# Moving start-up memsets, two loads and one copy in a fused strided-sparse attention and feed-forward kernel

## The chip, the cores and the metric

The kernel runs on one core of one Trainium2 chip. The metric is the device time of one execution in microseconds (us). A core has five engines that run their own instruction streams: TensorE (PE in the profile, its weight loads PEld), VectorE (DVE), ScalarE (ACT), GpSimd (POOL) and SyncE (SP, which here only issues transfers). Sixteen DMA engines move the data. GpSimd's loads go through the queue q0 of the profile, those of SyncE through q1, two of ScalarE's through q10.

## The reference

```python
# q, k, v: (batch 8, heads 8, seq 576, head_dim 64)
scores = (q @ k^T) / sqrt(64)
rel = pos[:, None] - pos[None, :]
local   = (rel >= 0) & (rel < 32)                       # heads 0 to 3
strided = (rel >= 0) & (pos_k % 32 == pos_q % 32)       # heads 4 to 7
attn = softmax(where(mask, scores, -1e9)) @ v
x = attn as (4608 tokens, 512)
h = x @ w_in                                            # (4608, 2048)
g = max(h, 0) + alpha * min(h, 0)                       # alpha per column of h
out = g @ w_out                                         # (4608, 512), float32
```

## The kernel before

The work of a batch is four *pairs* of heads: pairs 4b and 4b+1 are batch b's local heads, 4b+2 and 4b+3 its strided ones. A local pair is cut into six blocks of 96 queries against 128 keys, a strided pair into eight blocks of 72 by 72, because only positions with the same remainder attend to each other. For each pair `score_both` forms the scores on TensorE, ScalarE takes the exponential (L391, L400, L406), and GpSimd (for pair 11 VectorE) multiplies the mask in (L402, L409). `pv_piece` multiplies with V, whose 65th column of ones gives the sum of each row; VectorE takes its reciprocal (L437) and scales (L439) into a 16-bit tile x, for some strided pairs the fixed tile `x16s`. Then x is turned so that head dimensions lie on partitions, into `xT`, a ring of 1536 columns: either by TensorE (`x_piece`, L455, and a copy out of PSUM, L230 on ScalarE or L232 on VectorE) or by a DMA transpose from SyncE (`x_dma`: L472 for a local pair; L469 into `xs` for a strided one, which ScalarE then copies into `xT` at L478).

The feed-forward part works on nine chunks of 512 tokens. `lin1_piece(n, m)` multiplies one of 16 column blocks of w_in with chunk n (L613, four matmuls over the four pairs' 128 rows), ScalarE takes the negative part (L621), VectorE finishes the activation into `gT` (L624). `lin2_fast` is the second product (L709, L719) by seven products of halves instead of eight, for which sums of halves of g (`g_sum`, L653, on GpSimd or VectorE) and of w_out are formed. For chunk n, a loop of 30 steps i runs 16 steps of `lin1_piece` and 14 of `lin2_fast`; between them `attn_n` puts pieces of the attention of a later batch, taken from the list `pieces` in a fixed order. The step with the index g in that list has the scores of pair g, the products with V of pair g-1 and the turning of x of pair g-2; some of its pieces also cast or load the next batches' data. All instructions are kept in program order on each engine, so each engine's order is what this order of calls makes.

q and k of a batch's local heads reach SBUF as 32-bit tiles (`load_qk`, L104) and are cast to 16 bits (`cast_l`, L234 on GpSimd, L230 on ScalarE), then turned on TensorE (L292). From batch 5 on they come as rows (`load_rows`, L116) and are turned by DMA. The strided q and k come into `qsd` and `ksd` (`load_d`, L135) and are turned by DMA into `qT` and `kT` (`transpose_d`, L176). V comes by `load_v`: a local one straight into `vl` (L222), a strided one into `stv` (L212), from which `cast_v` copies it into `vs`. The weights come by `load_w` in four parts each (L762 for w_in into `win`, L758 for w_out).

At the start TensorE runs seventeen warm-up matmuls (L769) while the first loads run. VectorE and GpSimd set the constant parts of tiles with memsets; those of GpSimd stand before and after its first loads: two of `stv`, two of `vl`, four of `win`. The first three batches' pieces and chunk 0 are called from lists written out by hand; the loop described above begins with chunk 1.

Of the kernel before, what the change touches and what calls it, by code (L numbers as in the profile page):

```python
# [32 lines left out]
def kernel(  # L33
# [10 lines left out]
    nc = tc.nc  # L44
    keep = tc.keep_in_program_order
# [44 lines left out]
    x16s = cpool.tile([80, 1024], F16)  # L90
# [114 lines left out]
    def load_v(b, strided):  # L205


        if strided:
            st = spool.tile([128, 2048], F16, tag="v", bufs=2, name="stv")
            step = 2 if b == 0 else 4  # L210
            for h in range(0, 4, step):
                keep(nc.gpsimd.dma_start(  # L212
                    st[0:72, 512 * h : 512 * (h + step)].rearrange("p (h e) -> p h e", h=step),
                    v[b, 4 + h : 4 + h + step, :, :].rearrange("h (p t) d -> p h (t d)", t=8)))
            loaded[b] = st
        else:
            v16 = vls[b % 2]
            base = v[b, 0:1, 0:1, :]
            r0 = 32 if b < 2 else 0
            step = 12 if b == 0 else 24  # L220
            for c in range(0, 24, step):
                keep(nc.gpsimd.dma_start(  # L222
                    v16[r0:128, c : c + step, 0:64],
                    bass.AP(tensor=base.tensor, offset=base.offset + (96 * c - 32 + r0) * D,
                            ap=[[D, 128 - r0], [96 * D, step], [1, D]])))
            cast16[(b, False, "v")] = v16
# [271 lines left out]
    def X(g, eng=None):  # L498
        return lambda: x_piece(pairs[g], eng or ("act" if pairs[g].strided else "dve"))

    for g in range(7, npair + 2):
        c = g // 4
        a, p, t = g, g - 1, g + 1
        okA = 8 <= a < npair
        okP = 8 <= p < npair
        okT = 8 <= t < npair and t < 4 * NX and (t % 4 == 0 or t < 4 * DX and t % 2 == 0)
        nP = len(pairs[p].pgroups) if okP else 0
        seq = []
        if okA:
            seq.append(("S", lambda a=a: score_both(pairs[a])))  # L510
        if okP:
            seq.append(("P", Pv(p, 0)))
        if okT:
            seq.append(("T", T(t // 2, "q")))
        if 8 <= g - 2 < npair and not pairs[g - 2].xd:
            seq.append(("X", X(g - 2)))
        if okP:
            seq.append(("P", Pv(p, 1)))
        if okT:
            seq.append(("Tk", T(t // 2, "k")))  # L520
        if nP == 3:
            seq.append(("P", Pv(p, 2)))
        if g == 14:
            seq[0], seq[1] = seq[1], seq[0]
        if not seq:
            seq.append(("N", lambda: None))

        todo = [(c, pr) for pr in range(2)] if g % 4 == 0 and 8 < g < npair else []

        if g % 4 == 1 and 9 <= g and c + 1 < B:  # L530
            todo = [(c + 1, nm) for nm in "qk"]
        lastP = max([i for i, z in enumerate(seq) if z[0] == "P"], default=len(seq) - 1)
        nslots = [i for i, z in enumerate(seq) if z[0][0] != "S"] or list(range(len(seq)))
        for i, (kind, fn) in enumerate(seq):
            extra = []
            if todo and i in nslots:
                left = len([z for z in nslots if z >= i])
                cnt = -(-len(todo) // max(1, left))
                extra = [todo.pop(0) for _ in range(min(cnt, len(todo)))]

            def run(fn=fn, extra=extra, g=g, c=c, kind=kind, lastp=(i == lastP), first=(i == 0),
                    second=(i == min(1, len(seq) - 1))):
                fn()
                for b, pr in extra:
                    if pr in ("q", "k"):
                        if b == 3:
                            continue
                        if b < NX:
                            cast_l(b, pr)
                        if b + 1 < NX:  # L550
                            load_qk(b + 1, pr)
                        continue
                    if b == 3:
                        continue
                    cast_v(b, pr, "pool")
                    if pr == 1 and b + 1 < B:
                        load_v(b + 1, True)
                if first and g % 4 == 2 and NX <= c + 1 < B:
                    turn_rows(c + 1)
                if lastp and g % 4 == 3 and NX <= c + 2 < B:  # L560
                    load_rows(c + 2, "k")
                if lastp:
                    if 4 * DX <= g - 1 < npair and pairs[g - 1].xd:
                        x_dma(pairs[g - 1])
                    if g % 4 == 3 and DX < c + 1 < B:
                        transpose_d()
                    if g % 4 == 2 and DX < c and c + 1 < B:
                        load_d(c + 1)
                    if g % 4 == 1 and DX < c and c + 1 < B:
                        load_v(c + 1, False)  # L570
                    if g % 4 == 1 and NX <= c + 2 < B:
                        load_rows(c + 2, "q")
                if second and 4 * DX <= g - 3 < npair and pairs[g - 3].xd and pairs[g - 3].strided:
                    after.append(lambda: x_copy(pairs[g - 3]))
            feed(run, g - 2 if kind == "X" else -1)
# [180 lines left out]
    def load_w(c, second):  # L756
        if second:
            keep(nc.gpsimd.dma_start(  # L758
                wout16[:, 4 * c : 4 * c + 4, :],
                moe_w_out[512 * c : 512 * c + 512, :].rearrange("(kf p) c -> p kf c", p=128)))  # L760
        else:
            keep(nc.gpsimd.dma_start(  # L762
                win16[:, :, 512 * c : 512 * c + 512],
                moe_w_in[:, 512 * c : 512 * c + 512].rearrange("(kk p) c -> p kk c", p=128)))
# [25 lines left out]
    keep(nc.vector.memset(kTs[1], 0.0))  # L790
    for t in ets:
        keep(nc.vector.memset(t[:, 576:640], 0.0))
    keep(nc.vector.memset(kTs[0][:, :, 0:32], 0.0))
    keep(nc.vector.memset(kTs[0][:, :, 608:672], 0.0))
    for nm in "qk":
        keep(nc.vector.memset(qks[nm][64:80], 0.0))
    keep(nc.gpsimd.memset(x16s[64:80], 0.0))
    keep(nc.vector.tensor_copy(id32, ident[0:72, 0:72]))

    keep(nc.gpsimd.memset(vss[0][:, :, :, 64:65], 1.0))  # L800
    keep(nc.gpsimd.memset(vls[0][0:32, 0:1, 0:64], 0.0))
    keep(nc.gpsimd.memset(vls[0][:, :, 64:65], 1.0))
    load_v(0, True)
    load_v(0, False)
    for c in range(4):
        load_w(c, False)
    keep(nc.gpsimd.memset(vls[1][0:32, 0:1, 0:64], 0.0))
    keep(nc.gpsimd.memset(vls[1][:, :, 64:65], 1.0))
    keep(nc.gpsimd.memset(vss[1][:, :, :, 64:65], 1.0))
# [136 lines left out]
    for n in range(1, NCH):  # L946
        ab = attn_until(n + 1) if n + 1 < B else len(pieces)
        left = ab - pos["i"]
        acc = 0.0
        for i in range(30):  # L950
            if i < 16:
                lin1_piece(n, 8 * (i // 8) + 2 * (i % 4) + i % 8 // 4)
            else:
                lin2_fast(n, i - 16)
            held = []
            if n == 1 and i == 15:
                held.extend(late)
                late.clear()
            if n == 1:
                cnt = int(i > 12 or i in (0, 2, 4, 6, 9, 11))  # L960
            else:
                acc += left / (19.5 if n == B - 2 else 21) * (0.5 if i < 16 else 1.0)
                cnt = int(acc)
                acc -= cnt
            attn_n(cnt, ab)
            for fn in held:
                fn()
            if n == 2 and i == 8:
                load_v(4, True)
            for z, h, eng in {1: early, 2: sums2}.get(n, sums).get(i, ()):  # L970
                g_sum(n, z, h, eng)
            if n > 1:
                continue
            if i == 7:
                for pr in range(2):
                    cast_v(2, pr, "pool")
                    load_qk(4, "qk"[pr])
            if i == 4:
                load_v(3, True)
            if i == 15:  # L980
                load_v(3, False)
                load_d(3)
                cast_l(3, "q", "act")
            if i == 17:
                cast_l(3, "k", "act")
            if i == 24:
                for pr in range(2):
                    cast_v(3, pr, "pool")
        while pos["i"] < ab:
            attn_step(ab)  # L990
# [30 lines left out]
```

## Time and profile before

| | |
|---|---|
| runs | 295.78, 296.0, 297.6 us; median 296.0 |
| profiled execution | 297.99 us, of which the profile's span is 296.2 us |
| granted TensorE clock | 0.999 |
| busy, of the span | PE 98%, PEld 63%, DVE 73%, ACT 62%, POOL 62% |
| chain that ended last | PE 80%, DMA 11%, DVE 4%, POOL 2%, ACT 2% |
| share of the DMA engines by queue | q0 60.5%, q1 37.3%, q10 0.9% |

Times in the profile count from the start of the span. A row of a timeline gives start, length, engine, line of the kernel, operation, destination and sources, shape, and in brackets how long the engine had stood idle before it and what ended that. A row of waits gives the waiting instruction, what it waited for, and the total, the number and the longest of the waits. A row of the chain gives start, length and what the program's end hung on there. A row of stretches gives the stretch, its length, the busy time of PE, PEld, DVE, ACT and POOL with the number of instructions, the granted clock, the DMA engines' share and GB/s. A row of a DMA queue gives packets, MB and the time of its packets as a share of the sixteen engines in that stretch; a row of DMA issues gives their number, size and median time from issue to landing.

### The profile page before, as it was taken

The numbers are of one execution on the slowest core, as the hardware profiler recorded it, in microseconds if no ns is written. First come the engines' busy times: TensorE is split into PE (matmuls) and PEld (weight loads), VectorE is DVE, ScalarE is ACT, GpSimd is POOL, SyncE is SP. The second block draws the span as 40 slices with busy tenths as digits, with TensorE's granted clock in tenths as the row PEclk, the third lists the DMA queues.
The fourth block names the chain that finished last, engine by engine and source line by source line (L and its number), as shares of the span: only waits on it lengthen the run. The fifth ranks groups of instructions, "written<-read, shape, count | busy, mean of one in ns | idle before, by whom it ended". The sixth has DMA issues, their size and how long they took to land.

```text
span 296.2 us, 6949 instructions
## 1 busy us (share of the span) xinstructions
PE 289.4 (98%) x2732; PEld 187.5 (63%) x2732; DVE 215.2 (73%) x412; ACT 182.3 (62%) x337; POOL 183.1 (62%) x168
## 2 busy tenths in 40 slices
PE   8999999998999999999999999999999999999995
PEld 3754555644884478646864686468646964784584
DVE  4787886677965986588848984898489858926852
ACT  1767766896947775775477647764776267416630
POOL 9562538999479896979896987585463305002200
PEclk9999999999999999999999999999999999999999
DMA  7999999999997999997999999985611130022004
GB/s 186 260 189 201 199 240 254 163 189 284 197 103 134 197 156 132 211 146 127 151 204 124 134 140 185 159 115 104 180 20 23 49 117 0 0 73 71 0 2 143
DMA packets 97488, 41.18 MB, mean 139 GB/s; under 512 B 75360, under 2 KB 94256, under 8 KB 97456
## 3 DMA queue, kind: packets, MB, share of 16 engines
q0 software_dynamic: 51008, 17.77, 60.5%
q1 hardware_dynamic: 46096, 22.32, 37.3%
q10 hardware_dynamic: 352, 0.66, 0.9%
q8 instruction: 21, 0.34, 0.5%
q14 instruction: 11, 0.09, 0.1%
HBM read 38.24 MB, written 9.44 MB: 161 GB/s over the span
## 4 chain that ended last, share of the span: by engine, by line
PE 80%; DMA 11%; DVE 4%; POOL 2%; ACT 2%; issue 1%; SPq 0%; DVEq 0%; ACTq 0%; POOLq 0%
PE hps L613 38%; PE ops L719 20%; PE ops L709 8%; DMA win<-in_moe_w_in_dram 5%; PE ops L892 4%; DMA kT<-ksd 4%; PE pv L430 3%; DMA xs<-x16s 2%; PE sp L377 2%; DVE gsum L653 1%; PE ops L907 1%; PE tp L292 1%; PE sph L377 1%; PE xp L455 1%; DVE gT L624 1%
## 5 line engine op out<-in xcount | busy, mean ns | idle before, releaser
L613 PE MATMUL hps<-xT,win 128*128 128x512 f16 x576 | 132.9, 379 | 1.3 <-DMA win<-in_moe_w_in_dram 0.7
L624 DVE SCALAR_TENSOR_TENSOR gT<-neg,oma,hps 128x512 f16<-128x512 f32 x144 | 105.2, 744 | 37.6 <-ACT neg L621 30.1
L621 ACT ACTIVATE neg<-hps 128x512 f32<-128x512 f32 x144 | 85.8, 598 | 34.0 <-PE hps L613 31.3
L613 PEld LDWEIGHTS <-win 128*128 128x128 f16 x576 | 53.5, 98 | 59.4 <-issue 1.3
L653 POOL TENSOR_TENSOR gsum<-gT 128x1024 f16<-128x1024 f16 x15 | 31.9, 2124 | 41.7 <-DVE gT L624 36.7
L402 POOL TENSOR_TENSOR et<-et,consts 128x576 f16<-128x576 f16 (+1 forms) x23 | 32.5, 1414 | 31.0 <-ACT et L400 29.9
L719 PEld LDWEIGHTS <-gT 128*128 128x128 f16 x384 | 35.7, 98 | 6.1 <-issue 0.6
L439 DVE TENSOR_TENSOR x<-pv,rc 96x384 f16<-96x384 f32 (+2 forms) x62 | 33.0, 532 | 2.1
L719 PE MATMUL ops<-wout,gT 128*128 128x256 f16 x256 | 32.1, 273 | 0.1
L709 PE MATMUL ops<-wsum,gsum 128*128 128x256 f16 x248 | 30.7, 273 | 0.0
L409 POOL TENSOR_TENSOR et<-et,consts 128x576 f16<-128x576 f16 (+1 forms) x23 | 29.7, 1292 | 0.1
L430 PEld LDWEIGHTS <-et 72*128 72x128 f16 (+1 forms) x448 | 23.5, 98 | 8.6 <-ACT et L342 0.3
L400 ACT ACTIVATE et<-sp 128x576 f16<-128x576 f32 (+1 forms) x24 | 15.5, 645 | 17.1 <-PE sp L377 17.1
L719 PEld LDWEIGHTS <-gsum 128*128 128x128 f16 x256 | 23.7, 98 | 3.0
L709 PEld LDWEIGHTS <-gsum 128*128 128x128 f16 x256 | 23.7, 98 | 2.8
L437 DVE RECIPROCAL rc<-pv 72x6 f32<-72x6 f32 (+2 forms) x80 | 14.7, 184 | 10.5 <-PE pv L430 10.1
L664 DVE TENSOR_TENSOR osb<-ops,par 128x512 f32<-128x512 f32 (+1 forms) x15 | 10.1, 674 | 13.1 <-PE ops L719 9.4
L662 ACT COPY osb<-ops 128x512 f32<-128x512 f32 x16 | 9.4, 587 | 16.6 <-PE ops L719 16.4
L406 ACT ACTIVATE et<-sph 128x288 f16<-128x288 f32 (+1 forms) x48 | 18.9, 409 | 0.0
L736 ACT COPY par<-ops 128x512 f32<-128x512 f32 x15 | 8.8, 588 | 12.7 <-PE ops L709 12.2
L719 PE MATMUL ops<-wsum,gT 128*128 128x256 f16 x128 | 16.1, 272 | 0.1
L719 PE MATMUL ops<-wsum,gsum 128*128 128x256 f16 x128 | 16.2, 272 | 0.0
(113 smaller groups left out, 354.4 us busy)
## 6 DMA issues: line engine op xcount, KB each, us to landing
out_dram<-osb SPq DMA_DIRECT2D x35, 256.0 KB, 4.1
vl<-in_v_dram POOLq DMA_DIRECT2D x6, 384.0 KB, 9.9
win<-in_moe_w_in_dram POOLq DMA_DIRECT2D x4, 512.0 KB, 17.7
wout<-in_moe_w_out_dram POOLq DMA_DIRECT2D x4, 512.0 KB, 17.2
qsd<-in_q_dram POOLq DMA_DIRECT2D x7, 288.0 KB, 7.8
ksd<-in_k_dram POOLq DMA_DIRECT2D x7, 288.0 KB, 9.0
stv<-in_v_dram POOLq DMA_DIRECT2D x7, 288.0 KB, 6.9
ql<-in_q_dram SPq DMA_DIRECT2D x3, 576.0 KB, 7.4
```

The costliest lines, as they stand in the source:

```text
L400: keep(nc.scalar.activation(ev.rearrange("r (y c) -> r y c", y=2), sp[0:r, :, 0:n], AF.Exp, scale=SCALE))
L402: keep(mul(mv, mv, m, op=ALU.mult))
L406: keep(nc.scalar.activation(ev[:, n * y : n * y + n], sps[y][0:r, 0:n], AF.Exp, scale=SCALE))
L409: keep(mul(mv, mv, m, op=ALU.mult))
L430: keep(nc.tensor.matmul(pv[:, 65 * x : 65 * x + 65], et[0:r, c : c + 128], v16[0:r, 2 * P.pr + hh, t, :] if P.strided else v16[:, 6 * (2 * ...
L439: keep(nc.vector.tensor_tensor(P.x16[0:w, c0 : c0 + 64 * nb].rearrange("r (c e) -> r c e", e=64), pvv[:, :, 0:64], rc[0:w, 0:nb].unsqueeze ...
L613: keep(nc.tensor.matmul(hps, win16[:, kk, 128 * m : 128 * m + 128], xT[:, kk, c0 : c0 + 512], start=(kk == (0 if n > 1 else 2)), stop=(kk ...
L621: keep(nc.scalar.activation(neg, hps, AF.Relu, scale=-1.0))
L624: keep(nc.vector.scalar_tensor_tensor(gTs[n][:, m, :], neg, oma[:, m : m + 1], hps, op0=ALU.mult, op1=ALU.add))
L653: keep((nc.vector if eng == "dve" else nc.gpsimd).tensor_tensor(gsum[i][:, hs], a, b, op=op))
L709: keep(nc.tensor.matmul(o, gsum[i][:, y, 128 * z : 128 * z + 128], wsum[i][:, y, :], start=(x == "5" and y == 0 and (z == 0 or alone)), st ...
L719: keep(nc.tensor.matmul(o, lhs(y), rhs(y), start=(first and y == 0), stop=(y == 7), skip_group_check=True))
```

## The change

- Five memsets come to stand behind GpSimd's first eight loads: those on `vs`, one on `vl`, two on `kTs[0]`, which VectorE did, and the one on `x16s`.
- The strided V of batch 3 (`load_v(3, True)`) is issued at step 7 of chunk 1, ahead of the two copies of batch 2's V, instead of at step 4.
- The local q and k of batch 4 are loaded at step 22 of chunk 1 instead of step 7. On SyncE they then stand behind the turning of x of pairs 8, 9 and 10 and of batch 3's strided q and k, and ahead of the four stores of that chunk.
- GpSimd casts them at step 6 of chunk 2, behind a gate sum and ahead of pair 14's mask products, instead of within the attention pieces of g = 13, where the casts stood among pair 13's mask products.
- The turned x of pair 11 is copied out of PSUM by VectorE (L232) instead of ScalarE (L230).

TensorE's order does not change; SyncE, ScalarE, VectorE and GpSimd each have the named instructions elsewhere and the rest as it was.

```diff
@@ the list of attention pieces
-            seq.append(("X", X(g - 2)))
+            seq.append(("X", X(g - 2, "dve" if g == 13 else None)))
...
                     if pr in ("q", "k"):
-                        if b == 3:
+                        if b in (3, 4):
                             continue
                         if b < NX:
                             cast_l(b, pr)
@@ the start
-    keep(nc.vector.memset(kTs[0][:, :, 0:32], 0.0))
-    keep(nc.vector.memset(kTs[0][:, :, 608:672], 0.0))
...
-    keep(nc.gpsimd.memset(x16s[64:80], 0.0))
     keep(nc.vector.tensor_copy(id32, ident[0:72, 0:72]))
 
-    keep(nc.gpsimd.memset(vss[0][:, :, :, 64:65], 1.0))
-    keep(nc.gpsimd.memset(vls[0][0:32, 0:1, 0:64], 0.0))
     keep(nc.gpsimd.memset(vls[0][:, :, 64:65], 1.0))
     load_v(0, True)
     load_v(0, False)
     for c in range(4):
         load_w(c, False)
+    keep(nc.gpsimd.memset(vss[0][:, :, :, 64:65], 1.0))
+    keep(nc.gpsimd.memset(vls[0][0:32, 0:1, 0:64], 0.0))
+    keep(nc.gpsimd.memset(kTs[0][:, :, 0:32], 0.0))
+    keep(nc.gpsimd.memset(kTs[0][:, :, 608:672], 0.0))
+    keep(nc.gpsimd.memset(x16s[64:80], 0.0))
@@ the loop over chunks n and steps i
+            if n == 2 and i == 6:
+                for nm in "qk":
+                    cast_l(4, nm, "pool")
...
             if n > 1:
                 continue
             if i == 7:
+                load_v(3, True)
                 for pr in range(2):
                     cast_v(2, pr, "pool")
-                    load_qk(4, "qk"[pr])
-            if i == 4:
-                load_v(3, True)
+            if i == 22:
+                load_qk(4, "q")
+                load_qk(4, "k")
```

## The prediction

> **What bounds the kernel now.** I read the page first, then TensorE's own waits, then the chain of waits in order of time. The page says that PE is busy nearly throughout, so only what makes PE stand still is worth anything; PE's waits name the places where it does, and the chain says what lies behind each.
>
> ```profile
> span 296.2 us, 6949 instructions
> PE 289.4 (98%) x2732; PEld 187.5 (63%) x2732; DVE 215.2 (73%) x412; ACT 182.3 (62%) x337; POOL 183.1 (62%) x168
> ```
> ```profile
> PE sp L377 <- DMA kT<-ksd: 0.8, 1, 0.8
> PE hps L613 <- DMA win<-in_moe_w_in_dram: 0.7, 1, 0.7
> PE hps L613 <- ACT xT L230: 0.5, 1, 0.5
> ```
> ```profile
> 0.73 0.96 POOL x16s L797
> ...
> 5.29 15.04 DMA win<-in_moe_w_in_dram
> 20.38 0.60 PE hps L613 x2
> ...
> 22.55 9.13 PE hps L613 x42
> ...
> 60.59 10.45 DMA kT<-ksd
> 71.09 0.30 PE sp L377 x8
> ...
> 82.36 7.18 DMA xs<-x16s
> ...
> 90.41 0.55 ACT xT L478
> ...
> 91.39 2.10 PE hps L613 x9
> ...
> 108.85 1.75 PE ops L709 x16
> ```
>
> Besides the start itself these are PE's waits, and each stands behind a transfer: the first projection weights at 20.38, the turned strided k of batch 2 at 71.09, and pair 10's and pair 11's x at 91.39. Each of the edits aims at one of these three, so what they can bring is bounded by them: 0.7 and 0.8, and at 91.39 somewhat more than the 0.5 shown. There PE had begun a projection piece at 89.81 with three of its four matmuls:
>
> ```profile
> 88.65 0.55 DVE L439 TENSOR_TENSOR x<-pv,rc 96x384 f16<-96x384 f32 x1
> 88.68 0.42 PE L455 MATMUL xp<-consts,x 72*128 72x72 f16 x8
> 89.57 1.40 ACT L478 COPY xT<-xs 128x384 f16<-128x384 f16 x2 [1.53 <-DMA xs<-x16s]
> 89.81 1.12 PE L613 MATMUL hps<-xT,win 128*128 128x512 f16 x3
> 90.87 0.69 ACT L230 COPY xT<-xp 128x384 f16<-128x384 f16 x2
> 92.58 2.33 DVE L624 SCALAR_TENSOR_TENSOR gT<-neg,oma,hps 128x512 f16<-128x512 f32 x3 [3.38 <-ACT neg L621]
> ```
>
> Forty-two such matmuls took 9.13 us, 0.217 each, so three end at 90.46 and PE lost 91.39 - 90.46 = 0.93 us. From 91.39 on the chain is PE's own work again, so what is won here should stay won.
>
> **The change part by part.** *Memsets.* Ahead of GpSimd's first load stood x16s (0.96), one on vs and two on vl; one on vl stays. The first load goes from 1.95 to about 0.73 + 0.28 = 1.0, and all the loads behind it, the four of win last, go 0.95 earlier.
>
> ```profile
> 1.88 0.28 POOL L802 MEMSET vl<- 128x24 f16 x1
> 1.95 1.56 POOL L212 DMA_DIRECT2D stv<-in_v_dram  x2
> 8.39 0.36 POOL L809 MEMSET vs<- 128x32 f16 x1
> 11.72 1.28 POOL L234 CAST ql<-ql 128x640 f16<-128x640 f32 x2 [2.97 <-DMA ql<-in_q_dram]
> ```
>
> The memsets that stood behind the loads ended at 8.39 + 0.36 = 8.75, so now at 7.8; x16s, vs, vl and the two of kT that VectorE gave up join them, at 0.96 and four times 0.36 by the nearest row, 2.4 us in all, and they end by 10.2. The q cast waits for its load until 11.72 anyway, which hides them with 1.5 us to spare; without that cover they would push the cast and what PE turns from it. VectorE's saving counts as nothing: PE's first work after the warm-up waits for the constants, not for memsets. The weights do not gain 0.95 in full, because the DMA engines are shared. From 7 to 8 us GpSimd's queue (q0) moved its first 0.05 MB beside the hardware queue's loads of q and k:
>
> ```profile
> q0 software_dynamic: 83, 0.05, 30.3%
> ```
>
> If q0 starts 0.95 earlier with that share, it takes 0.95 x 30% = 0.3 us from the loads of q and k ahead of it. So the bounds are a loss of 0.3 (q and k later, win no earlier) and a gain of 0.7 (the whole wait). I take a gain of 0.3, nearer the middle, since the engines only have so much free time to give.
>
> *Strided V of batch 3.* Its issue (0.77) moves from between two mask products to just before the copies of batch 2's V.
>
> ```profile
> 63.63 0.77 POOL L212 DMA_DIRECT2D stv<-in_v_dram  x1
> 68.11 2.02 POOL L234 COPY vs<-stv 72x1024 f16<-72x1024 f16 x2
> ...
> 85.61 2.02 POOL L234 COPY vs<-stv 72x1024 f16<-72x1024 f16 x2
> ```
> ```profile
> q0 software_dynamic: 400, 0.30, 61.2%
> ```
>
> The last row is the DMA view of 68 to 71 us: q0 moved 0.30 MB with 61% of the engines just while kT, issued at 60.59, was ending. Four microseconds later they are out of its way. In the next stage the same turning landed 4.2 us after its issue, here 10.45; it need come only 0.8 sooner for PE not to wait. Bounds 0 and 0.8; I take 0.8, since nearly all of q0's bytes in that stretch go away. The V itself is copied at 85.61, seventeen microseconds after its new place; even the 15.04 us that win took at the start would be hidden. GpSimd's mask products for pairs 8 and 9 come up to 0.77 sooner, the copies of V at most 0.1 later.
>
> *Batch 4's q and k.* Two loads of 0.59 MB leave SP's queue ahead of the x turnings of pairs 8 and 9 and stand behind the turnings of pair 10's x and batch 3's strided q and k, ahead of four stores. At the rate of the first row below that frees 1.18 MB / 406 GB/s = 2.9 us of a full DMA stretch.
>
> ```profile
> 72.00:74.00 2.00, 2.00 (x24) 1.25 (x22) 0.84 (x2) 1.75 (x5) 1.98 (x3) 1.00 1.05 406
> 92.00:94.00 2.00, 2.00 (x16) 1.02 (x15) 1.42 (x2) 1.61 (x4) 2.00 (x3) 1.00 0.92 159
> ```
>
> Yet pair 10's x turning lies eight microseconds later, beside batch 3's local V, q and k on q0, which stay. I therefore leave its 7.18 us as they are. But it starts when VectorE has pair 10's x, and that chain begins at PE; with PE 0.3 + 0.8 earlier it is issued at 81.3, lands at 88.4, and ScalarE's first half of L478 (89.57 to 90.41, 0.84 long) ends at 89.3. PE then wants it at 89.81 + 2 x 0.217 - 1.1 = 89.1: 0.2 of waiting.
>
> The casts of batch 4's q and k (1.14 each) leave GpSimd's stretch at 88.82 and stand behind the gate sum that starts at 96.65:
>
> ```profile
> 88.82 1.14 POOL L234 CAST ql<-ql 128x1152 f16<-128x1152 f32 x1
> 96.65 2.14 POOL L653 TENSOR_TENSOR gsum<-gT 128x1024 f16<-128x1024 f16 x1
> 99.57 1.27 POOL L402 TENSOR_TENSOR et<-et,consts 72x576 f16<-72x576 f16 x1 [0.78 <-PE hps L613]
> 104.25 2.14 POOL L653 TENSOR_TENSOR gsum<-gT 128x1024 f16<-128x1024 f16 x1
> ```
>
> Behind them wait pair 14's two mask products, three load issues and the gate sum of 104.25. In the old clock the casts end at 98.79 + 2.28 = 101.07, the products start 1.5 late, and that gate sum ends at 107.9 instead of 106.39; PE reads it at 108.85. Cover 0.95 us, cost 0, if the loads are there. The k load must land by 101.07 - 1.14 + 0.95 = 100.9 of the old clock. It is issued behind the turning of k:
>
> ```profile
> 90.50 1.90 SPq L176 DMA_TRANSPOSE kT<-ksd  x1
> ```
> ```profile
> kT<-ksd SPq DMA_TRANSPOSE x1, 4.2
> ```
>
> That lands at 94.7, and at 406 GB/s the two loads are in at 97.6. PE is 1.8 ahead by then and the transfers perhaps 1.0 (their own wait is for batch 3's strided q, not for PE), so the limit is 100.9 - 1.8 + 1.0 = 100.1. It is met with 2.5 us to spare. The four stores are some 3 us later; nobody waits for them in this stage.
>
> *Pair 11's x on VectorE.* Its transposes end at 89.10, VectorE's own x at 89.20, and then VectorE is idle until 92.58; a copy of 576 columns took 0.45 there:
>
> ```profile
> 55.19 0.82 DVE L232 COPY xT<-xp 128x576 f16<-128x576 f16 x2
> ```
>
> Two pieces cost at most 0.9 and end by 90.1, hidden; ScalarE loses 0.69 of work behind L478, and PE's fourth matmul no longer waits for it. Of the 0.93 lost at 91.39 only the 0.2 above remains: 0.7.
>
> Sum: 0.3 + 0.8 + 0.7 = 1.8 us. The profiled execution took 297.99 with its span of 296.2, which becomes 296.2; the median of the runs was 296.0, 2.0 below it, and becomes 294.2.
>
> **Rivals.** (a) *Pair 10's x stays last.* The transfers beside it on q0 are not moved; if it lands at 89.55 whatever starts it, ScalarE's first half ends at 90.41, PE goes on at 90.45 instead of 91.39, and start and kT are swallowed: 0.94 gained, 295.1. For: q0 keeps V, q and k there. Against: its issue at 82.36 did wait for x16s, which hangs on PE.
>
> (b) *The late loads get half the engines.* Batch 4's q and k now run beside V's load and rows of batch 5 on q0. At 203 GB/s they take 5.8 us and land at 100.5; against a limit of 99.1 to 100.1 GpSimd is late by 0.4 to 1.4 and PE waits for the gate sum at its 108.85: 294.6 to 295.6, say 295.2. The Trainium skill (DMA: Bandwidth & Descriptors, Queues, rings and completion order) says that each engine goes round its queue rows packet by packet, a packet being some 9 to 17 descriptors; by that rule, with 128-byte pieces of V in one row, the two queues would come out near equal halves, and the sum would be this one. No stretch of this trace has such loads beside V, so nothing here bears it out or not.
>
> (c) *Slower: the k cast blocks GpSimd.* Same place, worse rate. In 95 to 104 us the stores shared the engines with V's load, and the hardware queue moved:
>
> ```profile
> q1 hardware_dynamic: 1531, 1.06, 52.4%
> ```
>
> That is 1.06 MB in 9 us, 118 GB/s, and all queues together made 159 at 92 to 94. At 159 the loads land at 102.1, at 118 at 104.7; less the limit of 100.1 PE stands 2.0 to 4.6 us at the gate sum, and with 1.8 gained the kernel is 0.2 to 2.8 slower, 297.5 in the middle. It decides from a landing 1.8 past the limit, 101.9, a rate of 164 GB/s. Against: nothing of 2.3 KB rows in q1 was that slow; 1 KB stores were.
>
> (d) *The DMA relief reaches further*: all three waits go wholly (0.7 + 0.8 + 0.93 = 2.4) and some of the stretches that ScalarE and VectorE hold up in between go too: 293.0 or less.
>
> **How the numbers follow.** Forecast 0.46 (own range 293.6 to 294.8: the start from 0 to 0.7, and run-to-run spread); (a) 0.19, (b) 0.14, (c) 0.14, (d) 0.07. The range of 293.3 to 297.4 takes in (a), (b) and half of (c), and leaves out (d). One per cent, about what a measurement of this kernel can tell from no change, is 3.0 us: faster than 293.0 is (d), 0.07; slower than 299.0 needs (c) at its end or something unseen, 0.07; within, 0.86.
>
> **What would show it.** Right: q0's first packets and win's landing earlier, PE's first projection matmul before 20.38; kT's landing before PE's score of pair 10 and no PE wait on kT; ScalarE's L478 no longer followed by L230, and a PE gap under 0.3 before the projection of the second chunk; GpSimd's casts of q and k without a DMA wait, gate sum before PE's L709. Wrong: a GpSimd wait on DMA kl near 97 to 103 and a PE wait on gsum (c); a PE wait on ScalarE's L478 of half a microsecond or more (a); the q cast at the start later than 11.72 and the whole front pushed.

## The result and the profile after

The change makes the kernel slower by 0.6%: a median of 297.99 us in 22 runs (296.46 to 301.87) against 296.01 in 22 runs of the kernel before (295.26 to 297.78); ratio 1.0062, 95% interval 1.0039 to 1.0086. A ratio leaves out executions far above a kernel's fastest, so it need not be that of the medians, and without its five runs at a granted clock of 0.993 or 0.994 the changed kernel's median would still be 297.65. Timed once more, beside other kernels (e9 below), the change came out at 1.0060 (1.0025 to 1.0094). The forecast was 294.2 us with a range up to 297.4: wrong in sign, and the range missed.

The profiled execution of the changed kernel took 297.95 us with a span of 296.2, by chance that of the profile before. First its page's head and TensorE's waits (total, number, longest):

```profile
span 296.2 us, 6947 instructions
PE 289.4 (98%) x2732; PEld 187.5 (63%) x2732; DVE 217.8 (74%) x412; ACT 181.5 (61%) x335; POOL 184.0 (62%) x170
```
```profile
PE wps L769 <- DVE wrm L789: 1.2, 1, 1.2
PE ops L709 <- POOL gsum L653: 0.9, 1, 0.9
PE ops L709 <- DVE gsum L653: 0.7, 1, 0.7
PE tf L154 <- DVE id L795: 0.3, 1, 0.3
```

The three waits at which the change aimed are not there, and two new ones of 0.9 and 0.7 us stand at the second product (L709), on the two gate sums. That the edits took the three away can't be read from this, as a second profile shows. It is of the *unchanged* kernel, in an execution of 295.79 us, near the median (e1 below):

```profile
span 294.0 us, 6949 instructions
```
```profile
PE wps L769 <- DVE wrm L789: 1.2, 1, 1.2
```

Here PE waits at the start and nowhere else. In the first profile of the kernel before, chunk 3 began with this row:

```profile
121.67 2.11 PE L613 MATMUL hps<-xT,win 128*128 128x512 f16 x9
```

In the second it begins at 119.47, 2.2 us earlier, which is the whole difference of their spans (296.2 and 294.0). So what made the first execution long lies ahead of that point, where the three waits, 2.0 us together, stood. Next, PE's timeline in the changed kernel and in this execution of the kernel before: the first matmul of chunk 2 and of chunk 3, and L709 between them.

```profile
88.46 1.24 PE L613 MATMUL hps<-xT,win 128*128 128x512 f16 x5
...
107.46 1.05 PE L709 MATMUL ops<-wsum,gsum 128*128 128x256 f16 x8 [0.89 <-POOL gsum L653]
109.25 1.05 PE L709 MATMUL ops<-wsum,gsum 128*128 128x256 f16 x8 [0.74 <-DVE gsum L653]
...
121.67 2.10 PE L613 MATMUL hps<-xT,win 128*128 128x512 f16 x9
```
```profile
88.45 1.33 PE L613 MATMUL hps<-xT,win 128*128 128x512 f16 x5
...
106.49 1.91 PE L709 MATMUL ops<-wsum,gsum 128*128 128x256 f16 x16
...
119.47 2.75 PE L613 MATMUL hps<-xT,win 128*128 128x512 f16 x12
```

At 88.4 the two are level: nothing was won up to there. Chunk 2 then takes 33.21 us instead of 31.02, 2.2 more, which is the difference of the medians (2.0) within the spread. From there to the end both take another 174.5 us, so between these two executions the whole loss lies in this one stretch; 1.63 of it are the two waits, the rest small steps behind them.

GpSimd's timeline of the stretch in the changed kernel, then in the kernel before (e1):

```profile
94.11 2.12 POOL L653 TENSOR_TENSOR gsum<-gT 128x1024 f16<-128x1024 f16 x1 [1.03 <-PE pv L430]
97.06 1.14 POOL L234 CAST ql<-ql 128x1152 f16<-128x1152 f32 x1 [0.83 <-DMA ql<-in_q_dram]
99.49 1.15 POOL L234 CAST kl<-kl 128x1152 f16<-128x1152 f32 x1 [1.29 <-DMA kl<-in_k_dram]
...
105.27 2.13 POOL L653 TENSOR_TENSOR gsum<-gT 128x1024 f16<-128x1024 f16 x1
107.36 1.27 POOL L402 TENSOR_TENSOR et<-et,consts 72x576 f16<-72x576 f16 x1
108.58 1.73 POOL L409 TENSOR_TENSOR et<-et,consts 72x576 f16<-72x576 f16 x1
```
```profile
95.27 2.15 POOL L653 TENSOR_TENSOR gsum<-gT 128x1024 f16<-128x1024 f16 x1
...
102.04 2.14 POOL L653 TENSOR_TENSOR gsum<-gT 128x1024 f16<-128x1024 f16 x1
...
105.36 1.27 POOL L409 TENSOR_TENSOR et<-et,consts 72x576 f16<-72x576 f16 x1
```

The casts stand in GpSimd's order and wait for their loads, 0.83 and 1.29 us. The gate sum behind them starts at 105.27 instead of 102.04: that is 2.28 for the casts and 2.12 for the waits, less 1.16 by which the first gate sum came earlier, 3.24 in all. It ends at 107.40, where PE wants it at 107.46 - 0.89 = 106.57.

Why the loads are late: the issues on SyncE's queue and their time to landing (the column before the landing time is the size), then the two queues from 92 to 99 us (packets, MB, share of sixteen engines).

```profile
87.40 1.99 SPq L176 DMA_TRANSPOSE kT<-ksd  x1
89.44 1.11 SPq L104 DMA_DIRECT2D ql<-in_q_dram  x1
90.60 0.61 SPq L104 DMA_DIRECT2D kl<-in_k_dram  x1
```
```profile
ql<-in_q_dram SPq DMA_DIRECT2D x1, 576.0 KB, 7.6
kl<-in_k_dram SPq DMA_DIRECT2D x1, 576.0 KB, 8.8
...
kT<-ksd SPq DMA_TRANSPOSE x1, 4.5
```
```profile
q1 hardware_dynamic: 736, 1.37, 67.0%
q0 software_dynamic: 2132, 0.27, 60.2%
```

They land at 97.0 and 99.4. The turned k ahead of them had landed at 87.40 + 4.5 = 91.9, so their 1.18 MB took 7.5 us, 157 GB/s, where the prediction gave them 2.9 us. From 92 to 99 us q1 as a whole, with some of the stores behind the loads, moved 1.37 MB, 196 GB/s, beside 0.27 MB of q0's small pieces that held the engines nearly as long. That is half the 406 GB/s of the prediction's row. The Trainium skill (DMA: Bandwidth & Descriptors, Queues, rings and completion order) has each engine go round the queue rows packet by packet; the trace fits that, with 67.0 and 60.2% of the engines' time for the two queues and 196 GB/s for q1, against 406 where it had the engines to itself.

VectorE's own gate sum, in the changed kernel and before (e1), is the second wait:

```profile
105.88 3.31 DVE L653 TENSOR_TENSOR gsum<-gT 128x1024 f16<-128x1024 f16 x1
...
111.39 0.68 DVE L653 TENSOR_TENSOR gsum<-gT 128x1024 f16<-128x1024 f16 x1
```
```profile
105.96 1.24 DVE L653 TENSOR_TENSOR gsum<-gT 128x1024 f16<-128x1024 f16 x1
```

By itself the sum takes 0.68. In the changed kernel it starts while GpSimd's late gate sum runs and ends at 109.19, 0.56 after the mask product behind it (107.36 + 1.27 = 108.63). Before, it starts while L409 runs and ends at 107.20, 0.57 after that one (105.36 + 1.27 = 106.63). So both times it ended nearly its own length after a GpSimd operation had ended, and in the changed kernel it had two of them ahead of it. The Trainium skill (SBUF — State Buffer, Who interferes with whom) says that a VectorE instruction with two inputs in SBUF contends with a GpSimd instruction that reads SBUF; the trace agrees, with 3.31 against 0.68 us.

### The profile page after: what moved, and what is told of

The parts are those of the page before. It is cut to its first block, busy times and chain, and to the rows that moved or that the text cites. A ratio compares the mean times of both kernels' runs of the same rounds, so it can differ in the third digit from the quotient of the medians.

```text
span 296.2 us, 6947 instructions
## 1 busy us (share of the span) xinstructions
PE 289.4 (98%) x2732; PEld 187.5 (63%) x2732; DVE 217.8 (74%) x412; ACT 181.5 (61%) x335; POOL 184.0 (62%) x170
## 4 chain that ended last, share of the span: by engine, by line
PE 90%; DVE 3%; DMA 2%; ACT 2%; issue 1%; SPq 0%; DVEq 0%; ACTq 0%
PE hps L613 40%; PE ops L719 22%; PE ops L709 9%; PE pv L430 4%; PE ops L892 4%; PE sp L377 2%; DMA consts<-consts 2%; PE xp L455 1%; PE sph L377 1%; PE ops L907 1%; DVE gsum L653 1%; PE tp L292 1%; DVE gT L624 1%; PE tf L154 1%; ACT neg L621 1%
## 5 line engine op out<-in xcount | busy, mean ns | idle before, releaser
L709 PE MATMUL ops<-wsum,gsum 128*128 128x256 f16 x248 | 30.9, 273 | 1.8 <-POOL gsum L653 0.9
L409 POOL TENSOR_TENSOR et<-et,consts 128x576 f16<-128x576 f16 (+1 forms) x23 | 30.1, 1310 | 0.1
L709 PEld LDWEIGHTS <-gsum 128*128 128x128 f16 x256 | 23.5, 98 | 5.2 <-DVE gsum L653 1.3
```

The costliest lines, as they stand in the source:

```text
L409: keep(mul(mv, mv, m, op=ALU.mult))
L709: keep(nc.tensor.matmul(o, gsum[i][:, y, 128 * z : 128 * z + 128], wsum[i][:, y, :], start=(x == "5" and y == 0 and (z == 0 or alone)), st ...
```

## The experiments

Chunk 2 below is the time from its first projection matmul to that of chunk 3 in the profile, beside PE's waits in it. Each group of four shares its runs of the kernel before, with medians of 296.2, 296.42 and 296.21 us.

| kernel | batch 4's loads | memsets | median | lowest | ratio (95%) | chunk 2 (PE waits in it) |
|---|---|---|---|---|---|---|
| e1_same | early | before | 296.02 | 295.35 | 0.9974 (0.9951-0.9996) | 31.02 (0) |
| e2_no_qk4 | early | moved | 296.32 | 295.76 | 0.9989 (0.9967-1.0011) | 30.97 (0) |
| e3_qk4_only | late | before | 297.34 | 295.45 | 1.0022 (0.9992-1.0053) | not used |
| e4_start_only | early | moved | 296.18 | 295.53 | 0.9994 (0.9969-1.0019) | 32.64 (x 0.9, 0.5) |
| e5_early_load | early | moved | 296.04 | 295.58 | 0.9983 (0.9963-1.0003) | 34.59 (kT 2.7, x 0.7) |
| e6_gsum_dve | late | moved | 296.78 | 296.07 | 1.0010 (0.9989-1.0032) | 32.37 (gate sum 0.6, gT 0.3) |
| e7_late_cast | late | moved | 297.11 | 296.64 | 1.0009 (0.9988-1.0029) | 32.10 (gate sum 0.3, cast 0.2) |
| e8_no_start | late | before | 296.95 | 295.73 | 1.0010 (0.9982-1.0037) | 33.16 (gate sums 0.7, 0.7) |
| e9_after_again | late | moved | 298.39 | 296.33 | 1.0060 (1.0025-1.0094) | 34.34 (gate sums 1.4, 0.7; x 0.5) |
| e10_stv_dve | early | before | 296.26 | 295.73 | 0.9993 (0.9973-1.0014) | 31.44 (x 0.3) |
| e11_early_no_start | early | before | 297.56 | 295.73 | 1.0026 (0.9995-1.0057) | not used |

The profiled executions of e3 and e11 took 300.2 and 300.27 us, 2.9 and 2.7 above their medians, so their chunk 2 is not compared.

**e1_same**: the kernel before, unchanged, profiled once more and timed against itself.

> The kernel before, unchanged, for a second profile of it and for what two equal kernels differ by. Theory A (the profile I argued from was an execution 2 us longer than the median, and its waits on kT and xs belong to that execution): ratio 1.000 within 0.3%, span 294.0 to 294.6, PE's waits on kT and on pair 10's and 11's x together under 0.6 us instead of 1.3. Theory B (those waits are in every execution and the change removes them): the same waits again, 0.8 and 0.5 us, whatever the span.

The profiled execution took 295.79 us and has none of the three waits (the row is above): an execution near the median can be without them. Two equal kernels came out at 0.9974, with an interval that just leaves out 1: what lies within some 0.4% here is not read as a difference.

**e12_same_again**: the kernel before, one more look.

> A third profile of the kernel before. If its waits on kT and xT belong to rarer executions: span 293.8 to 294.8 and none of them. If about every second execution has them: 50 to 50 that they are seen, with a span near 296.

This execution took 299.07 us, and PE's waits are back, larger than in the profile shown first:

```profile
PE hps L613 <- ACT xT L478: 2.1, 1, 2.1
PE sp L377 <- DMA kT<-ksd: 0.5, 1, 0.5
PE hps L613 <- ACT xT L230: 0.5, 1, 0.5
```
```profile
kT<-ksd SPq DMA_TRANSPOSE x1, 10.2
xs<-x16s SPq DMA_TRANSPOSE x1, 9.1
```

The same kernel, then, with the same work: 0, 2.0 and 3.1 us of PE's waits on transfers and on x in executions of 295.79, 297.99 and 299.07 us. Pair 10's x took 6.3, 7.2 and 9.1 us to be turned in these three.

**e2_no_qk4**: the changed kernel without its batch 4 part.

```diff
-                        if b in (3, 4):
+                        if b == 3:
...
-            if n == 2 and i == 6:
-                for nm in "qk":
-                    cast_l(4, nm, "pool")
...
-            if i == 22:
-                load_qk(4, "q")
-                load_qk(4, "k")
+                    load_qk(4, "qk"[pr])
```

> The changed kernel with batch 4's q and k loaded and cast where they were; memsets, strided V and VectorE's copy as changed. Theory 1 (the late loads make GpSimd wait 0.8 and 1.3 us for q and k, its gate sum comes late and with it VectorE's, and this costs about 3 us): no PE wait on gsum near 107, and 294.0 to 296.0. Theory 2 (the start costs, since TensorE's first work began 0.4 us later, and the late loads cost nothing): 297.5 to 298.5 as the changed kernel.

The loss is gone (0.9989, an interval clear of the changed kernel's), and so are both waits on the gate sums; chunk 2 is back at 30.97. GpSimd's gate sum starts at 102.47 and VectorE's takes 1.36. What remains of the change neither gains nor loses: the forecast's 1.8 us were not to be had.

**e3_qk4_only** and **e8_no_start**: the batch 4 part alone; the whole change without the memsets.

```diff
+    keep(nc.vector.memset(kTs[0][:, :, 0:32], 0.0))
+    keep(nc.vector.memset(kTs[0][:, :, 608:672], 0.0))
...
+    keep(nc.gpsimd.memset(x16s[64:80], 0.0))
...
+    keep(nc.gpsimd.memset(vss[0][:, :, :, 64:65], 1.0))
+    keep(nc.gpsimd.memset(vls[0][0:32, 0:1, 0:64], 0.0))
```

(The diff is e8's, against the changed kernel; e3 has also the strided V and pair 11's copy as before.)

> The kernel before with only batch 4's q and k loaded and cast where the change puts them. Theory 1: GpSimd waits for both loads, PE waits for gsum near 107 to 110, 297.0 to 299.5. Theory 2: 295.5 to 296.5.

> The changed kernel with the memsets where they were; strided V, VectorE's copy and batch 4's q and k as changed. If the start edit is neutral: 297.4 to 298.4, as the changed kernel, with PE's waits on gsum. If the start edit costs what is left over: 296.4 to 297.2.

Both medians are above that of before, by 1.1 and 0.5 us, but both intervals take in 1. e8's median of 296.95 lies in the range named for a start edit that costs something, not in that of a neutral one. Yet e8's profile, of an execution 1.3 us above that median, has the same stall as the changed kernel, 0.7 + 0.7 of PE waiting and a chunk of 33.16, with the loads late in the same way:

```profile
99.85 1.15 POOL L234 CAST kl<-kl 128x1152 f16<-128x1152 f32 x1 [1.97 <-DMA kl<-in_k_dram]
```
```profile
106.43 3.13 DVE L653 TENSOR_TENSOR gsum<-gT 128x1024 f16<-128x1024 f16 x1
```

The lowest times differ, though: 295.45 and 295.73 as the kernel before, where the changed kernel never came under 296.33. Without the moved memsets some executions seem to escape the stall; that these miss it was not seen in a profile, and what the memsets have to do with it is not shown.

**e4_start_only** and **e10_stv_dve**: the memsets alone; the strided V and pair 11's copy alone.

> The kernel before with only the memsets moved. Theory 1: 295.3 to 296.3, the first projection matmul at 19.9 to 20.4 as in the changed kernel, no more than 0.5 us gained. Theory 2: 297.0 to 298.0, with the first work of TensorE 0.4 us later.

> The kernel before with strided V of batch 3 later and pair 11's x copied by VectorE, and nothing else. If these two edits win something in a usual execution: 294.8 to 295.6, no PE wait on kT or xT. If they only take waits out of the rarer slow executions: median as before within 0.2%, fewer runs above 297.

They came out at 0.9994 and 0.9993: neither does anything by itself. The theory that the start alone costs the time falls, and the gains forecast for the two are not there either.

**e5_early_load**: the changed kernel with batch 4's loads back at step 7, the casts still at step 6 of chunk 2. It tells the late loads from the new place of the casts.

```diff
-            if i == 22:
-                load_qk(4, "q")
-                load_qk(4, "k")
+                    load_qk(4, "qk"[pr])
```

> The changed kernel with batch 4's q and k loaded early again (step 7 of chunk 1) and still cast by GpSimd at step 6 of chunk 2. Theory L (the late landing of the loads is what costs): GpSimd has no wait for ql and kl near 96 to 100, its gate sum ends by 105.5, PE does not wait for it, 295.3 to 296.6. Theory P (the place of the casts costs, 2.3 us of GpSimd's work ahead of the mask products and the gate sum, whenever the loads land): PE still waits for gsum near 107, 297.2 to 298.5.

The ratio is 0.9983, and the loss is gone. GpSimd's timeline shows the casts in their new place without a wait:

```profile
97.28 1.14 POOL L234 CAST ql<-ql 128x1152 f16<-128x1152 f32 x1
98.37 1.14 POOL L234 CAST kl<-kl 128x1152 f16<-128x1152 f32 x1
```

So the loss goes with the loads' landing, not with the casts' place. One reservation: PE stood 2.7 us on a turned k just then in this execution, which gave the gate sums time; that the place is free rests on the times, and e11, the same kernel with the memsets as before, is less clear (1.0026).

**e6_gsum_dve**: the changed kernel with that gate sum on VectorE, so that it no longer stands behind the casts.

```diff
-        5: [(2, 0, "pool")], 9: [(0, 0, "pool")], 15: [(0, 1, "dve")],
+        5: [(2, 0, "pool")], 9: [(0, 0, "dve")], 15: [(0, 1, "dve")],
```

> The changed kernel with the one gate sum of chunk 2 that GpSimd forms behind the casts (step 9) given to VectorE; loads and casts as changed, so GpSimd still waits for both loads. Theory G (the lateness reaches TensorE through that gate sum and nothing else): PE has no wait on gsum near 107 to 110, VectorE's sums take about 0.7 to 1.3 us each and none 3.3, 295.5 to 296.8. Rival M (the mask products of pairs 14 and 15 behind the casts hold TensorE too): PE waits for their products with V instead, 297.3 or more.

The ratio is 1.0010, and chunk 2 is 0.84 shorter than in the changed kernel with the k and q loads as late as ever:

```profile
98.44 1.14 POOL L234 CAST ql<-ql 128x1152 f16<-128x1152 f32 x1 [1.79 <-DMA ql<-in_q_dram]
100.56 1.70 POOL L234 CAST kl<-kl 128x1152 f16<-128x1152 f32 x1 [0.99 <-DMA kl<-in_k_dram]
```
```profile
100.58 0.68 DVE L653 TENSOR_TENSOR gsum<-gT 128x1024 f16<-128x1024 f16 x1
...
106.86 1.89 DVE L653 TENSOR_TENSOR gsum<-gT 128x1024 f16<-128x1024 f16 x1
```

So in this profile the waiting casts hurt through the gate sum behind them. The times do not tell it: e8, with both waits in its profile, has the same ratio. Of PE's waiting 0.6 stays, which had been excluded: VectorE's second sum now stands behind GpSimd's mask product (1.89). The sum that the edit moved takes 0.68, and here it is GpSimd's k cast beside it that is longer, 1.70 instead of 1.15.

**e7_late_cast**: the changed kernel with the casts at step 10, behind that gate sum.

```diff
-            if n == 2 and i == 6:
+            if n == 2 and i == 10:
```

> The changed kernel with the two casts at step 10 of chunk 2, behind GpSimd's gate sum instead of ahead of it; loads late as changed. Theory L or G: GpSimd finds both loads landed, its gate sum ends near 104, PE does not wait for gsum; the turning of q on PE near 105 may wait up to 0.6 us for its cast: 295.8 to 296.8. Rival M: the mask products of pair 15, now behind the casts, hold PE: 297.5 to 298.5.

GpSimd waits for no load and its gate sum starts at 101.78, yet PE loses 0.3 at VectorE's sum and 0.2 at the first turning of q:

```profile
101.78 2.14 POOL L653 TENSOR_TENSOR gsum<-gT 128x1024 f16<-128x1024 f16 x1
103.85 1.15 POOL L234 CAST ql<-ql 128x1152 f16<-128x1152 f32 x1
104.94 1.14 POOL L234 CAST kl<-kl 128x1152 f16<-128x1152 f32 x1
106.05 1.27 POOL L402 TENSOR_TENSOR et<-et,consts 72x576 f16<-72x576 f16 x1
```
```profile
105.68 2.19 DVE L653 TENSOR_TENSOR gsum<-gT 128x1024 f16<-128x1024 f16 x1
```

Its twelve runs lie close, 296.64 to 297.87; the lowest is 1.3 above e1's. The median of 297.11 lies between the two ranges that had been named. The ratio, 1.0009, is unclear; chunk 2 is 1.1 us longer than in e1.

**e9_after_again**: the changed kernel once more, in the company of e10 to e12.

> The changed kernel again, for a second profile and on the same chip as the next two. If the late loads meet GpSimd in every execution: PE's waits on GpSimd's and VectorE's gsum again, 1.0 to 2.0 us together, GpSimd's waits for ql and kl again, ratio 1.003 to 1.008. If they do so in some executions alone: no such waits, span near 294.

The ratio is 1.0060, and the same two waits are there (1.4 and 0.7). Over all the groups 27 of its 34 runs are above 297.0 us, and 27 of 122 of the kernel before.

**e11_early_no_start**: early loads and the memsets as before, with the late casts, the later strided V and pair 11's copy.

> The changed kernel with batch 4's loads early and the memsets where they were; strided V, VectorE's copy and the late casts as changed. The version that the runs so far point to: 295.2 to 296.2, no PE wait on gsum; a ratio under 0.998 only if the edits kept win something, 1.000 if they are neutral.

The ratio is 1.0026, unclear, and the median lies above the range named: half of its twelve runs are 295.73 to 296.82, half 298.3 to 301.77. In the profiled execution (300.27 us) PE does not wait for a gate sum, but 2.3 us for the turned k of batch 3, and right behind that the granted clock is near 0.5 for three microseconds. It is no better version. None was found that beats the kernel before by more than two equal kernels differ.

## Why the prediction was wrong

**The sum stood on the wrong execution.** "The profiled execution took 297.99 with its span of 296.2, which becomes 296.2; the median of the runs was 296.0, 2.0 below it, and becomes 294.2": this is the step that failed first. The three waits were what made that execution long. Subtracting 1.8 from the median took away waits that an execution at the median does not have (e1). With batch 4's part left out, the medians of e2, e4 and e10 are 296.18 to 296.32: a gain of nothing. That the profile lay 2.0 above the median was in plain sight; it should have been asked what those 2.0 were before anything was taken off.

*Memsets, 0.3.* GpSimd's first load moved from 1.95 to 1.35, not 1.0; 0.42 us of issue stood ahead of it. The first projection matmul, in the changed kernel's timeline and in e1's:

```profile
19.92 0.60 PE L613 MATMUL hps<-xT,win 128*128 128x512 f16 x2
```
```profile
19.87 0.59 PE L613 MATMUL hps<-xT,win 128*128 128x512 f16 x2
```

The 20.38 shown first was that execution's. The memsets are hidden, as said. The gain is 0.

*Strided V, 0.8.* The mechanism was right: kT lands after 7.9 to 8.7 us in the nine profiles with the V later, after 9.1 to 10.5 in the five with it where it was. The landing in the changed kernel and in e1:

```profile
kT<-ksd SPq DMA_TRANSPOSE x1, 8.0
```
```profile
kT<-ksd SPq DMA_TRANSPOSE x1, 9.1
```

At 9.1 PE did not wait for kT either. The gain is 0 in a usual execution; that it helps long ones was not shown.

*Pair 10's and 11's x, 0.7.* VectorE's copy is hidden as said, and PE's wait at the start of chunk 2 is gone. In e1 there was none: chunk 2 begins at 88.45, and at 88.46 after the change. The gain is 0; and in e9 the changed kernel too waits 0.5 us there. With no gain, rivals (a) and (d) fall too.

*Batch 4's loads, 0.* This is the second step that failed: "at 406 GB/s the two loads are in at 97.6", "with 2.5 us to spare". From the landing of the turned k they took 7.5 us instead of 2.9, 157 GB/s, which is near the 159 of rival (c) and not the 203 of (b). That they landed at 99.4, as (b)'s 100.5 less 1.0 would have it, is chance: the turned k was issued at 87.40, 3.1 earlier than 90.50 and not 1.0. The limit was off as well: with PE where it is in a usual execution the cast should have begun 0.89 before its 99.49, at 98.6, not at a limit of 99.1 to 100.1. So what (c) named as the sign of being wrong came: GpSimd waited for the k load, the gate sum came late and PE stood there. It stood 0.9 and not 2.0 to 4.6 us, and no gain of PE's stood against it; that (c)'s 297.5 lies near the 297.99 is two errors that cancel.

*What no case had.* Both (b) and (c) let PE wait for GpSimd's gate sum alone, 0.9 us here. VectorE's sum came to run beside it, took 3.31 instead of 1.24 and cost another 0.74. The prediction followed GpSimd's queue to the gate sum, but not what VectorE runs beside it then.

**Open**: why the changed kernel loses 0.6% where e3 and e8, with the same late loads, come out 0.1 to 0.2% above the kernel before, with intervals that reach below 1; the moved memsets are all that e8 lacks, and alone they do nothing (e4). So the late loads are needed for the loss (e2, e5), but that they are enough for it is not shown, nor how much of the 0.6% the stall in chunk 2 makes. Also open is what lengthens the DMA turnings from one execution to the next.

## What to carry to other kernels

Before a sum is made, compare the profiled execution with the median of the runs: if it lies above, find which waits make the difference, take them out of what may be won, and look at a second profile of the same kernel where that can be had. When a load is moved later, follow the engine that reads it: everything behind the waiting instruction in that engine's order is late too, and then what another engine runs beside it. A rate for a moved load is taken from a stretch in which the same other queue is busy, not from the fastest stretch of the trace.

## What the runs showed of the hardware

- VectorE's gate sum of 128x1024 takes 0.68 us by itself. The one of the timelines above ended 0.55 to 0.57 us after the end of one of GpSimd's operations in every profile in which GpSimd computed beside it: of the one under way or just beginning (0.99 to 1.36, and 1.89 us in all), or, where another followed that one at once, of that other (2.19, 3.13, 3.31; 3.80 in e9, 3.56 in e3). A mask product that came next paid for it, with 1.73 instead of 1.27. It is not always VectorE that pays: in e6 a gate sum that began with GpSimd's k cast took its 0.68, and the cast 1.70 instead of 1.15.
- DMA turnings of one size and place differ from execution to execution: kT 9.1 to 10.5 us, pair 10's x 6.3 to 9.1 us in the three profiles of the kernel before.
- A profiled execution is often not a usual one: of the fourteen here nine lay 0.7 to 3.6 us above the median of their kernel's runs, and none more than 0.5 below.
- TensorE's granted clock can fall for a few microseconds within an execution. In e11 it was 0.76 from 99 to 100 us, 0.50 to 102 and 0.54 to 103, right behind PE's wait of 2.28 us, and eight projection matmuls took 3.30 us instead of 1.90. In e5 PE stood 2.73 us at the same place and the clock stayed at 1.00, so the wait alone does not decide it.
